# Fewer, wider band matmuls, another order of the first loads, and the third conv slot moved to the stage border

## The chip, the cores and the metric

The kernel runs on one core of one Trainium2 chip. The time is device microseconds of one execution; the figure for the kernel before is the median of three executions, 521.17 us (521.16 to 522.0). Engines are named as in the profile: PE (TensorE, matmuls), PEld (its weight loads), DVE (VectorE), ACT (ScalarE), POOL (GpSimd), SP (SyncE, which here only issues transfers). POOL and SP each issue transfers from a list of their own, in program order; ACT can issue some too.

## The reference

A causal depthwise convolution of seven taps, whose weights are a softmax over the taps and differ per head (8 heads of 24 channels), is followed by a gated feed-forward block. Cut to what is computed:

```python
# x: (8, 3904, 192) float32, weight: (8, 7)
w = softmax(weight, axis=-1)                       # (sum + 1e-9 below)
x_pad = concatenate([zeros((B, 6, D)), x], axis=1)
out = einsum('hk,bskhg->bshg', w, windows_of_7(x_pad))
x = out.reshape(31232, 192)
a, b = x @ w1, x @ w2                              # 192 -> 1024
h = (a * b) @ w3                                   # 1024 -> 1024
return h @ w_out                                   # 1024 -> 192, float32
```

Nothing nonlinear stands between `w3` and `w_out`, so the kernel multiplies these two once and uses the product `W_sb` (1024 x 192).

## The kernel before, in words

**Tokens.** The 31,232 tokens are two streams (r = 0 and 1) of 15,616, which lie on partitions 0 to 63 and 64 to 127. The convolution works on windows of 64 input rows that give 58 output rows. Windows are grouped in 12 blocks (`SIZES`: 6, 4, 8, 10, 8, six of 36, and 20 windows). The feed-forward part works on 31 rounds R of 512 tokens per stream, in groups of four rounds.

**Convolution.** A head's seven taps become a banded 64 x 64 matrix. `band` (L245) builds the bands: DVE multiplies shifted diagonals by the tap weights (L247, tile `cprod`), PE sums the seven products through an identity (L256), and ACT or DVE casts the sum to `Aband` (`put`, L479). One call makes the bands of one head pair for both streams. `conv` (L274) then takes, for each head, four 64 x 64 matmuls (two halves of the block by two streams, L290) and casts the result to `convo` (L311, or L476 through `move` in the opening).

**First product.** `first_part` (L403) makes one part of 128 of the 1024 columns: a factor a by `wd[0]` and a factor b by `wd[1]` (six matmuls each, L381, 64 rows by 128 columns of the array, one per stream), an ACT cast of a to `asb` (L389), and a DVE multiply of `asb` by b into `abT` (L400). **Second product** (L420): 32 matmuls per round and stream (L432), a cast to `osb` (ACT, L437), and an output store.

**PSUM.** Four pairs of banks go round through the list `free`: `banks()` takes the first, `drained(p)` appends it behind the copy that empties it. So every PE result waits until the pair that it gets has been emptied.

**Order.** The program is scheduled by hand: each engine runs its instructions in the order in which the source writes them. After the opening come the four first products of group 0 with the small blocks' convolutions between them, then the product of `w3` and `w_out` (L467), and then for every group the eight second products, followed by the four first products of the next group. In each stage of second products one block is convolved, in three slots (heads 0 to 2, 3 to 5, 6 and 7) that stand behind the second products with index 1, 3 and 5 (4, 5 and 6 in the first stage, where block 5 has the slots 0, 1 and 2). The last slot also issues the block's store to `rows` in DRAM on SP; SP's transposes (L363) later bring these rows back as `xT`.

**The opening.** SP loads the first quarter of both weights as float32 into `wfirst` (L164), and ACT and POOL cast it into the two partition halves of `wd` (`cast_w`). The other quarters are loaded by POOL with a cast on the way (`load_w`, L169) and copied to the upper half by POOL (`copy_w`, L190). POOL's list begins with block 0's x for stream 0 (L172), two selects that make the diagonal `diag` (L176), block 0's x for stream 1, block 0's first rows (L182), block 1's x (L119), and the second quarter of the weights. ACT issues the load of the tap weights `wall` (L137).

**The pace.** In front of block 5's and 6's x loads POOL copies two elements of `w3T` into a scratch tile `pace` (L557). The copy waits for one of the transposes that bring `w3` in, and so it holds back all that POOL issues behind it.

Of the kernel before, what the change touches and what calls it, by code (L numbers as in the profile page):

```python
# [8 lines left out]
FP32 = mybir.dt.float32  # L9
BF16 = mybir.dt.bfloat16  # L10
AX = mybir.AxisListType
ALU = mybir.AluOpType
# [4 lines left out]
def kernel(  # L17
# [10 lines left out]
    nc = tc.nc  # L28

    B, S, D = x.shape  # L30
    H, K = weight.shape
    G = D // H
    DFF = moe_w1.shape[1]
    JT = DFF // 128
# [6 lines left out]
    GROUP = 4  # L41
    RING = GROUP * CH
    Q = 64
    ST = Q - PAD
    NP = D // Q
# [5 lines left out]
    NB = len(SIZES)  # L51
# [10 lines left out]
    work = ctx.enter_context(tc.tile_pool(name="work", bufs=2))  # L62
# [6 lines left out]
    free = list(range(NPAIR))  # L69
# [12 lines left out]
    def slot(shape, dtype, name):  # L82
        return stage.tile(shape, dtype, tag="slot", bufs=5, name=name)
# [21 lines left out]
    def load_x(b, parts=(0, 1)):  # L105
        tiles = xb_of.setdefault(b, [])
        zeros_of = zero_rows.setdefault(b, [])
        for i0, n in [v for e, v in enumerate(halves_of(b)) if e in parts]:
            xb = work.tile([128, n, D], BF16, tag="xb", bufs=5, name="xb")
            w = 0  # L110
            while w < n:
                i = i0 + w
                m = min(n - w, WB - i % WB)
                at_end = i + m == NWIN
                if at_end:
                    m -= 1
                if m:
                    for r in range(NS):
                        nc.gpsimd.dma_start(out=xb[Q * r:Q * r + Q, w:w + m, :],  # L119
                                            in_=x_spans(r, i, m))  # L120
                if i % WB == 0:
                    zeros_of += [(xb, 0, w), (xb, 1, w)]
                w += m
                if at_end:
                    nc.gpsimd.memset(xb[Q:128, w, :], 0.0)
                    t = tok(NWIN - 1) - PAD
                    nc.gpsimd.dma_start(out=xb[0:Q, w, :], in_=x_rows[t:t + Q, :])
                    nc.gpsimd.dma_start(out=xb[Q:Q + PAD + LAST, w, :],
                                        in_=x_rows[TS + t:TS + t + PAD + LAST, :])
                    w += 1  # L130
            if len(halves_of(b)) == 1:
                tiles += [(xb, 0), (xb, SIZES[b] // 2)]
            else:
                tiles.append((xb, 0))

    wall = const.tile([1, H, K], FP32)
    nc.scalar.dma_start(out=wall, in_=weight.rearrange("(o h) k -> o h k", o=1))  # L137

    n0 = SIZES[0] // 2
    xb0 = work.tile([128, 2 * n0, D], BF16, tag="xb", bufs=5, name="xb")  # L140
    xb_of[0] = [(xb0, 0), (xb0, n0)]
    wfirst = work.tile([Q, 2, NP, DFF // 4], FP32, tag="abT", bufs=GROUP, name="wfirst")
    pace = const.tile([1, 2], BF16)
    tiny = const.tile([128, 1], FP32)
    ones = const.tile([128, 1], BF16)
    zeros = const.tile([128, 128], BF16)
    half = const.tile([1, 3 * Q], BF16)
    ident = const.tile([128, 128], BF16)
    diag = const.tile([128, Q + PAD], BF16)
    nc.vector.memset(zeros, 0.0)  # L150
    nc.vector.memset(tiny, 0.0)
    nc.vector.memset(ones, 1.0)  # L152
    nc.vector.memset(xb0[:, 0, :], 0.0)
    nc.vector.memset(half, 0.0)
    nc.vector.memset(half[:, Q:2 * Q], 1.0)
# [3 lines left out]
    WC = (0, DFF // 4, DFF // 2, DFF * 3 // 4, DFF)  # L159
    wd = [const.tile([128, NP, DFF], BF16, name=f"wd{i}", tag=f"wd{i}") for i in range(2)]  # L160
    w_rows = [w.rearrange("(k q) f -> q k f", q=Q) for w in (moe_w1, moe_w2)]

    for i in range(2):
        nc.sync.dma_start(out=wfirst[:, i], in_=w_rows[i][:, :, 0:WC[1]])  # L164

    def load_w(part):
        cs = slice(WC[part], WC[part + 1])
        for i in range(2):
            nc.gpsimd.dma_start(out=wd[i][0:Q, :, cs], in_=w_rows[i][:, :, cs])  # L169

    def load_x0(r):
        nc.gpsimd.dma_start(out=xb0[Q * r:Q * r + Q, 1:, :], in_=x_spans(r, 1, 2 * n0 - 1))  # L172

    load_x0(0)
    for p0 in (0, Q):
        nc.gpsimd.affine_select(  # L176
            out=diag[p0:p0 + Q], in_=ones[p0:p0 + Q].to_broadcast([Q, Q + PAD]),
            pattern=[[-1, Q + PAD]], compare_op=ALU.is_equal, fill=0.0, base=0,
            channel_multiplier=1)
    load_x0(1)  # L180
    for r in range(NS):
        nc.gpsimd.dma_start(out=xb0[Q * r + PAD:Q * r + Q, 0, :],  # L182
                            in_=x_rows[r * TS:r * TS + ST, :])
    load_x(1)
    def cast_w(i, r, f):
        f(out=wd[i][Q * r:Q * r + Q, :, 0:WC[1]], in_=wfirst[:, i])

    def copy_w(part, i, f):
        cs = slice(WC[part], WC[part + 1])
        f(out=wd[i][Q:128, :, cs], in_=wd[i][0:Q, :, cs])  # L190

    load_w(1)
    cast_w(1, 1, nc.gpsimd.tensor_copy)
    load_w(2)
    load_x(2)
    for i in range(2):
        copy_w(1, i, nc.gpsimd.tensor_copy)
# [5 lines left out]
    def warm(n):  # L203
        p, t = banks()
        for j in range(n):
            nc.tensor.matmul(t[:, j % 2, :], zeros, zeros[:, 0:1].to_broadcast([128, CH]),  # L206
                             start=True, stop=True)
        drained(p)

    warm(6)  # L210

    wmax = const.tile([1, H], FP32)
    wsum = const.tile([1, H], FP32)
# [1 line left out]
    wsb = const.tile([128, 2, 2, K], BF16)  # L215
    nc.vector.reduce_max(out=wmax, in_=wall, axis=AX.X)
    nc.vector.tensor_tensor(
        out=wall, in0=wall, in1=wmax.unsqueeze(2).to_broadcast([1, H, K]), op=ALU.subtract)
# [5 lines left out]
        out=wrow, in0=wall, in1=wsum.unsqueeze(2).to_broadcast([1, H, K]), op=ALU.mult)  # L224
# [11 lines left out]
    Aband = const.tile([128, 2, 2, 2, Q], BF16)  # L236

    def band_of(h, r):
        return Aband[Q * r:Q * r + Q, h // 4, (h % 4) // 2, int(h % 2 != r), :]

    d0 = diag[:, 0:1]
    taps = bass.AP(tensor=d0.tensor, offset=d0.offset,
                   ap=[list(d0.ap[0]), [1, K], [1, Q]])

    def band(g, e):  # L245
        c = slot([128, K, Q], BF16, "cprod")
        nc.vector.tensor_tensor(  # L247
            out=c, in0=taps, in1=wsb[:, g, e].unsqueeze(2).to_broadcast([128, K, Q]),
            op=ALU.mult)
        p, bps = banks()  # L250
        for k in range(K):
            for v in range(2):
                for r in range(2):
                    rs = slice(Q * r, Q * r + Q)
                    o = Q * (r ^ v)
                    nc.tensor.matmul(bps[o:o + Q, v, 0:Q], ident[rs, rs], c[rs, k, :],  # L256
                                     start=(k == 0), stop=(k == K - 1))
        return p, Aband[:, g, e], bps[:, :, 0:Q]


    xT = [const.tile([128, RING + Q], BF16, name=f"xT{k}", tag=f"xT{k}") for k in range(NP)]

# [140 lines left out]
    def first_part(R, fts, c0, c1):  # L403
        a, b = (first_factor(R, i, fts, c0, c1) for i in range(2))
        first_times(R, fts, c0, c1, first_cast(*a), *b)
# [1 line left out]
    def first_tile(R):  # L407
        abT_of[R] = work.tile([128, JT, NS, CH], BF16, tag="abT", bufs=GROUP, name="abT")

    def first_product(R, between=None, fts=range(JT)):  # L410
        if R not in abT_of:
            first_tile(R)
        N = width(R)
        step = CH // N
        for ft in fts[::step]:
            first_part(R, list(range(ft, ft + step)), 0, N)
            if between and ft in between:
                between[ft]()

# [33 lines left out]
    w3T = const.tile([128, JT, DFF], BF16)  # L453
# [24 lines left out]
    def put(f, p, dst, src):  # L478
        f(out=dst, in_=src)  # L479
        drained(p)  # L480

    cast_w(0, 0, A)
    put(A, *band(0, 0))
    put(A, *band(0, 1))
    cast_w(0, 1, A)
    made = [band(1, 0), band(1, 1)]
    put(V, *made[0])
    put(V, *made[1])
    cast_w(1, 0, A)

    def move_all(p, moves, fs):
        for f, m in zip(fs, moves):
# [41 lines left out]
    def need(R):  # L534
        return next(i for i in range(NWIN) if tok(i) >= (R + 1) * CH)
# [18 lines left out]
        3: seq([(pe_transposes, 4)])})  # L554
    store(4, need(GROUP - 1) - 1, queue=nc.gpsimd)
    nc.gpsimd.dma_start(out=wo_b, in_=wor)
    P(out=pace, in_=w3T[0:1, JT // 2 - 1, DFF - 2:DFF])  # L557
    load_x(5)
    load_x(6)
    first_product(3)  # L560
# [11 lines left out]
    slots = (range(0, 3), range(3, 6), range(6, H))  # L572
# [6 lines left out]
    for p, rounds in enumerate(groups):  # L579
        b = PROLOGUE_BLOCKS + p  # L580
        order = rounds[-1:] + rounds[:-1] if rounds[-1] == NR - 1 else rounds
        for j, R in enumerate(order if p else ()):
            first_product(R)
            send(R + GROUP)
            if j < 2 and b < NB:
                P(out=pace, in_=abT_of[R][0:1, JT - 1, 1, 0:2])  # L586
                load_x(b, (j,))
        if b < NB:
            zero(b)
        at = {1: [(b, slots[0])], 3: [(b, slots[1])], 5: [(b, slots[2])]}  # L590
        if p == 0:
            at = {0: [(5, slots[0], (V, A))], 1: [(5, slots[1], (V, A))],
                  2: [(5, slots[2], (V, A), need(GROUP))], 4: at[1], 5: at[3], 6: at[5]}
        for i, (R, r) in enumerate((R, r) for R in rounds for r in range(NS)):
            second_product(R, r, R == NR - 1 and r == 1, nc.sync if p else nc.gpsimd)
            for c in at.get(i, ()) if b < NB else ():
                conv_heads(*c)
            if p == 0 and i == 2:
                send(2 * GROUP - 1)
# [31 lines left out]
```

## Time and profile before

| | us |
|---|---|
| median of three executions | 521.17 |
| the profiled execution | 522.07 |
| its span, first to last instruction | 520.4 |
| PE busy | 513.5 (99%) |
| DVE busy | 357.5 (69%) |
| ACT busy | 325.7 (63%) |
| POOL busy | 58.4 (11%) |
| granted TensorE clock, mean over the span | 1.000 |

The span is shorter than the execution's time, because the profile counts from the first to the last instruction of the program. The rows of the profile read: start and length in us (timeline and chain), engine, line of the kernel, operation, output<-inputs, shapes, and in brackets the idle time of the engine ahead of the row and what ended it. "SPq" or "ACTq" is an engine's issuing side, which does not count as busy. The chain is followed back from the last instruction; each piece of it is either work or the wait for what released the next piece.

### The profile page before, as it was taken

How to read it: one execution, taken by the hardware profiler on the slowest of the kernel's cores; microseconds unless marked ns; L12 is line 12 of the kernel's file. 1: busy time of each engine (PE TensorE's matmuls, PEld its weight loads, DVE VectorE, ACT ScalarE, POOL GpSimd, SP SyncE). 2: the span in 40 equal slices, each digit the busy share in tenths (PEclk: the TensorE clock that was granted, in tenths of full speed). 3: DMA queues.
4: the chain of work that ended last, by engine and by line, in shares of the span. 5: the costliest groups of instructions: out<-in, count | busy, mean ns of one | idle time of the engine just before them, and what ended most of it. 6: DMA issues, size and time to landing. Idle time of an engine off the chain costs nothing.

```text
span 520.4 us, 13006 instructions
## 1 busy us (share of the span) xinstructions
PE 513.5 (99%) x5576; PEld 339.8 (65%) x5576; DVE 357.5 (69%) x343; ACT 325.7 (63%) x410; POOL 58.4 (11%) x98
## 2 busy tenths in 40 slices
PE   8999999999999999999999999999999999999997
PEld 4455788455885558845588455884558855599567
DVE  6778646899538994389943899438993299911970
ACT  6887643777437774377743777337774377734762
POOL 8501522130000200002000010001200000000000
PEclk9999999999999999999999999999999999999999
DMA  9979998699656973569645699456724532024004
GB/s 116 169 142 126 163 222 208 162 186 166 143 146 161 116 94 113 146 161 128 82 116 147 155 122 89 118 146 157 103 44 122 155 96 32 17 94 151 1 3 152
DMA packets 133420, 64.61 MB, mean 124 GB/s; under 512 B 90304, under 2 KB 132642, under 8 KB 133298
## 3 DMA queue, kind: packets, MB, share of 16 engines
q1 hardware_dynamic: 94320, 44.06, 36.1%
q0 software_dynamic: 38896, 19.62, 30.4%
q8 instruction: 43, 0.70, 0.6%
q14 instruction: 15, 0.12, 0.1%
q10 hardware_dynamic: 146, 0.10, 0.1%
HBM read 33.25 MB, written 36.52 MB: 134 GB/s over the span
## 4 chain that ended last, share of the span: by engine, by line
PE 95%; ACT 1%; DVE 1%; DMA 1%; POOL 1%; issue 0%; POOLq 0%; ACTq 0%
PE pairs L381 59%; PE pairs L432 32%; PE pairs L290 3%; DVE abT L400 1%; PE pairs L467 1%; ACT asb L389 1%; DMA xb<-in_x_dram 1%; PE pairs L343 0%; POOL xb L172 0%; POOL xb L182 0%; ACT convo L311 0%; POOL xb L119 0%; ACT xT L355 0%; POOL diag L176 0%; PE pairs L507 0%
## 5 line engine op out<-in xcount | busy, mean ns | idle before, releaser
L400 DVE TENSOR_TENSOR abT<-asb,pairs 128x1024 bf16<-128x1024 bf16 (+1 forms) x245 | 298.1, 1217 | 76.8 <-ACT asb L389 60.5
L381 PE MATMUL pairs<-xT,wd 64*128 64x512 bf16 (+3 forms) x3000 | 319.7, 371 | 0.7 <-DVE abT L400 0.3
L389 ACT CAST asb<-pairs 128x1024 bf16<-128x1024 f32 (+1 forms) x245 | 247.1, 1009 | 67.7 <-PE pairs L381 67.3
L381 PEld LDWEIGHTS <-wd 64*128 64x128 bf16 x3000 | 162.3, 94 | 151.8 <-issue 1.8
L432 PE MATMUL pairs<-W_sb,abT 128*128 128x192 bf16 x1952 | 166.1, 246 | 0.0
L432 PEld LDWEIGHTS <-abT 128*128 128x128 bf16 x1952 | 159.6, 98 | 9.7 <-issue 9.7
L437 ACT COPY osb<-pairs 128x384 f32<-128x384 f32 x122 | 58.3, 478 | 116.0 <-PE pairs L432 116.0
L311 DVE CAST convo<-pairs 128x864 bf16<-128x864 f32 (+5 forms) x67 | 50.8, 815 | 67.6 <-PE pairs L290 67.6
L119 POOL DMA_DIRECT2D xb<-in_x_dram x42 | 32.2, 781 | 7.6 <-PE pairs L381 4.1
L586 POOL COPY pace<-abT 1x2 bf16<-1x2 bf16 x10 | 1.7, 174 | 238.7 <-DVE abT L400 238.7
L290 PE MATMUL pairs<-xb,Aband 64*64 64x432 bf16 (+5 forms) x384 | 17.5, 284 | 0.4 <-DMA xb<-in_x_dram 0.3
L290 PEld LDWEIGHTS <-Aband 64*64 64x64 bf16 x384 | 7.2, 106 | 7.5 <-issue 6.3
L311 ACT CAST convo<-pairs 128x512 bf16<-128x512 f32 (+4 forms) x15 | 8.1, 584 | 0.5 <-PE pairs L290 0.4
L444 POOL DMA_DIRECT2D out_dram<-osb x8 | 6.1, 758 | 18.4 <-ACT osb L437 18.4
L437 DVE COPY osb<-pairs 128x192 f32<-128x192 f32 x1 | 0.4, 358 | 11.1 <-PE pairs L432 11.1
L467 PEld LDWEIGHTS <-w3T 128*128 128x128 bf16 x64 | 5.2, 98 | 0.4 <-issue 0.4
L467 PE MATMUL pairs<-wo_b,w3T 128*128 128x192 bf16 x64 | 5.5, 246 | 0.0
L190 POOL COPY wd<-wd 64x768 bf16<-64x768 bf16 x6 | 4.8, 847 | 0.0
L206 PE MATMUL pairs<-zeros 128*128 128x512 bf16 x8 | 3.7, 615 | 1.1 <-DVE ones L152 1.1
L343 PE MATMUL pairs<-ident,convo 128*128 128x128 bf16 x48 | 3.9, 219 | 0.7 <-DVE convo L476 0.5
L343 PEld LDWEIGHTS <-convo 128*128 128x128 bf16 x48 | 2.9, 97 | 2.5 <-issue 1.6
L469 ACT CAST W_sb<-pairs 128x192 bf16<-128x192 f32 x8 | 2.6, 320 | 2.8 <-PE pairs L467 2.8
(52 smaller groups left out, 38.6 us busy)
## 6 DMA issues: line engine op xcount, KB each, us to landing
out_dram<-osb SPq DMA_DIRECT2D x52, 384.0 KB
xb<-in_x_dram POOLq DMA_DIRECT2D x18, 432.0 KB, 7.8
rows<-convo SPq DMA_DIRECT2D x8, 648.0 KB
out_dram<-osb POOLq DMA_DIRECT2D x8, 384.0 KB, 4.9
w3rows<-in_moe_w_dram POOLq DMA_DIRECT2D x2, 1024.0 KB, 12.0
xb<-in_x_dram POOLq DMA_DIRECT2D x6, 240.0 KB, 5.4
rows<-convo SPq DMA_DIRECT2D x4, 324.0 KB
xT<-rows SPq DMA_TRANSPOSE x81
```

What stands on the lines that cost most here:

```text
L119: nc.gpsimd.dma_start(out=xb[Q * r:Q * r + Q, w:w + m, :], in_=x_spans(r, i, m))
L190: f(out=wd[i][Q:128, :, cs], in_=wd[i][0:Q, :, cs])
L290: nc.tensor.matmul(view(slice(Q * c, Q * c + Q), r)[:, :, j * G:(j + 1) * G], band_of(h, r), xb[Q * r:Q * r + Q, w0:w0 + n, h * G:(h + 1) ...
L311: f[e % len(f)](out=dst, in_=part)
L343: nc.tensor.transpose(out=tps[:, w, :], in_=convo[:, w, k].rearrange("p r g -> p (r g)"), identity=ident)
L381: nc.tensor.matmul(p[:, r, e * n:e * n + n], wd[i][rs, k, ft * 128:(ft + 1) * 128], xT[k][rs, r0 + c0:r0 + c1], start=(k == 0), stop=(k == ...
L389: nc.scalar.copy(out=asb, in_=pa)
L400: nc.vector.tensor_tensor(out=dst, in0=asb, in1=pb, op=ALU.mult)
L432: nc.tensor.matmul(ops[:, (g - g0) * D:(g - g0) * D + D], ab[:, jt, r, g * 128:(g + 1) * 128], W_sb[:, jt, :], start=(jt == 0), stop=(jt = ...
L437: f(out=osb[:, g0:g0 + per, :].rearrange("p g d -> p (g d)"), in_=ops[:, 0:per * D])
L444: queue.dma_start(out=out[t0:t0 + ng * 128, :].rearrange("(g p) d -> p g d", p=128), in_=osb)
L467: nc.tensor.matmul(wps[:, 0, 0:D], w3T[:, gt, jt * 128:(jt + 1) * 128], wo_b[:, gt, :], start=(gt == 0), stop=(gt == JT - 1))
```

## The change

- **Bands.** `bands(g)` takes the place of two calls of `band(g, e)`: two DVE multiplies write the two head pairs side by side into one `cprod` tile, and each of the 28 matmuls has 128 columns instead of 64. There are 56 such matmuls instead of 112, and two casts of 256 elements (one on ACT, one on DVE) instead of four of 128. `Aband`'s axes change their order to suit.
- **First loads.** SP loads the tap weights and then the first quarter of the first weight alone. The second weight's first quarter is loaded by POOL with a cast, behind block 0's x and ahead of block 1's; POOL copies it to the upper half behind the issues of the second and third quarters. POOL's cast and one ACT cast go.
- **Selects.** POOL sets `ones` itself and runs the selects ahead of all its loads. One of six warm-up matmuls goes.
- **Pace.** The copy that holds block 5's x reads what the second transpose of `w3`'s second half brings, not the fourth.
- **Border.** In the stages of second products the third slot stands behind index 7, the last one, instead of index 5 (6 in the first stage), and its two heads are cast by DVE and ACT, one each, instead of both by DVE. In the first product behind such a border, two entries of `free` are exchanged behind the second part.

```diff
-    nc.scalar.dma_start(out=wall, in_=weight.rearrange("(o h) k -> o h k", o=1))
+    nc.sync.dma_start(out=wall, in_=weight.rearrange("(o h) k -> o h k", o=1))
...
-    wfirst = work.tile([Q, 2, NP, DFF // 4], FP32, tag="abT", bufs=GROUP, name="wfirst")
+    wfirst = work.tile([Q, NP, DFF // 4], FP32, tag="abT", bufs=GROUP, name="wfirst")
...
-    nc.vector.memset(ones, 1.0)
...
-    for i in range(2):
-        nc.sync.dma_start(out=wfirst[:, i], in_=w_rows[i][:, :, 0:WC[1]])
+    nc.sync.dma_start(out=wfirst, in_=w_rows[0][:, :, 0:WC[1]])
...
-    load_x0(0)
+    nc.gpsimd.memset(ones, 1.0)
     for p0 in (0, Q):
         nc.gpsimd.affine_select(
...
+    load_x0(0)
     load_x0(1)
     for r in range(NS):
         nc.gpsimd.dma_start(out=xb0[Q * r + PAD:Q * r + Q, 0, :],
                             in_=x_rows[r * TS:r * TS + ST, :])
+    load_w(0, (1,))
     load_x(1)
...
     load_w(1)
-    cast_w(1, 1, nc.gpsimd.tensor_copy)
     load_w(2)
+    copy_w(0, 1, nc.gpsimd.tensor_copy)
     load_x(2)
...
-    warm(6)
+    warm(5)
...
-    def band(g, e):
-        c = slot([128, K, Q], BF16, "cprod")
-        nc.vector.tensor_tensor(
-            out=c, in0=taps, in1=wsb[:, g, e].unsqueeze(2).to_broadcast([128, K, Q]),
-            op=ALU.mult)
+    def bands(g):
+        c = slot([128, K, 2, Q], BF16, "cprod")
+        for e in range(2):
+            nc.vector.tensor_tensor(
+                out=c[:, :, e, :], in0=taps,
+                in1=wsb[:, g, e].unsqueeze(2).to_broadcast([128, K, Q]), op=ALU.mult)
...
-                    nc.tensor.matmul(bps[o:o + Q, v, 0:Q], ident[rs, rs], c[rs, k, :],
+                    nc.tensor.matmul(bps[o:o + Q, v, 0:2 * Q], ident[rs, rs],
+                                     c[rs, k].rearrange("p e s -> p (e s)"),
                                      start=(k == 0), stop=(k == K - 1))
...
-    def first_product(R, between=None, fts=range(JT)):
+    def first_product(R, between=None, fts=range(JT), behind_conv=False):
...
             first_part(R, list(range(ft, ft + step)), 0, N)
+            if behind_conv and ft == step:
+                free[1], free[2] = free[2], free[1]
...
-    cast_w(0, 0, A)
-    put(A, *band(0, 0))
-    put(A, *band(0, 1))
-    cast_w(0, 1, A)
-    made = [band(1, 0), band(1, 1)]
-    put(V, *made[0])
-    put(V, *made[1])
-    cast_w(1, 0, A)
+    A(out=wd[0][0:Q, :, 0:WC[1]], in_=wfirst)
+    put(A, *bands(0))
+    A(out=wd[0][Q:128, :, 0:WC[1]], in_=wfirst)
+    put(V, *bands(1))
...
-    P(out=pace, in_=w3T[0:1, JT // 2 - 1, DFF - 2:DFF])
+    P(out=pace, in_=w3T[0:1, 1, DFF - 2:DFF])
...
-            first_product(R)
+            first_product(R, behind_conv=j == 0 and b <= NB)
...
-        at = {1: [(b, slots[0])], 3: [(b, slots[1])], 5: [(b, slots[2])]}
+        at = {1: [(b, slots[0])], 3: [(b, slots[1])], 7: [(b, slots[2], (V, A))]}
         if p == 0:
             at = {0: [(5, slots[0], (V, A))], 1: [(5, slots[1], (V, A))],
-                  2: [(5, slots[2], (V, A), need(GROUP))], 4: at[1], 5: at[3], 6: at[5]}
+                  2: [(5, slots[2], (V, A), need(GROUP))], 4: at[1], 5: at[3], 7: at[7]}
```

More of the change, by code (lines that the diff above doesn't have):

```diff
@@ L161, with load_w @@
     w_rows = [w.rearrange("(k q) f -> q k f", q=Q) for w in (moe_w1, moe_w2)]
-    for i in range(2):
-        nc.sync.dma_start(out=wfirst[:, i], in_=w_rows[i][:, :, 0:WC[1]])
-    def load_w(part):
+    nc.sync.dma_start(out=wfirst, in_=w_rows[0][:, :, 0:WC[1]])
+    def load_w(part, which=(0, 1)):
         cs = slice(WC[part], WC[part + 1])
-        for i in range(2):
+        for i in which:
             nc.gpsimd.dma_start(out=wd[i][0:Q, :, cs], in_=w_rows[i][:, :, cs])
@@ L183 @@
                             in_=x_rows[r * TS:r * TS + ST, :])
+    load_w(0, (1,))
     load_x(1)
-    def cast_w(i, r, f):
-        f(out=wd[i][Q * r:Q * r + Q, :, 0:WC[1]], in_=wfirst[:, i])
     def copy_w(part, i, f):
@@ L238, in band_of @@
     def band_of(h, r):
-        return Aband[Q * r:Q * r + Q, h // 4, (h % 4) // 2, int(h % 2 != r), :]
+        return Aband[Q * r:Q * r + Q, h // 4, int(h % 2 != r), (h % 4) // 2, :]
     d0 = diag[:, 0:1]
@@ L255, in band @@
                     o = Q * (r ^ v)
-                    nc.tensor.matmul(bps[o:o + Q, v, 0:Q], ident[rs, rs], c[rs, k, :],
+                    nc.tensor.matmul(bps[o:o + Q, v, 0:2 * Q], ident[rs, rs],
+                                     c[rs, k].rearrange("p e s -> p (e s)"),
                                      start=(k == 0), stop=(k == K - 1))
-        return p, Aband[:, g, e], bps[:, :, 0:Q]
+        return p, Aband[:, g].rearrange("p v e s -> p v (e s)"), bps[:, :, 0:2 * Q]
     xT = [const.tile([128, RING + Q], BF16, name=f"xT{k}", tag=f"xT{k}") for k in range(NP)]
```

## The prediction
> **What bounds the kernel now.** I read the page's busy line first, then the chain of work that ended last, then the timeline of the three places that the change touches: the opening, the end of the first weight stage, and a border between two stages.
>
> ```profile
> span 520.4 us, 13006 instructions
> PE 513.5 (99%) x5576; PEld 339.8 (65%) x5576; DVE 357.5 (69%) x343; ACT 325.7 (63%) x410; POOL 58.4 (11%) x98
> ...
> L400 DVE TENSOR_TENSOR abT<-asb,pairs 128x1024 bf16<-128x1024 bf16 (+1 forms) x245 | 298.1, 1217 | 76.8 <-ACT asb L389 60.5
> ```
>
> TensorE (PE) is busy for all but 6.9 us, so only stalls, tile switches and the opening can be won. The profiled execution took 522.07 us (span 520.4 and 1.67 around it); the median of the runs is 521.17, so I add my sum to that median. The chain, in order of time:
>
> ```profile
> 5.19 4.20 DMA xb<-in_x_dram
> 9.39 0.04 issue
> 9.43 0.44 PE pairs L290 x31
> ...
> 67.44 0.30 PE pairs L290 x3
> 67.74 0.01 issue
> 67.75 0.70 PE pairs L290 x9
> 68.46 2.75 PE pairs L432 x32
> 71.20 0.67 PE pairs L290 x12
> ...
> 149.62 0.49 PE pairs L290 x8
> 150.10 5.39 PE pairs L432 x64
> 155.49 41.55 PE pairs L381 x384
> ```
>
> Before 9.39 the chain is POOL's list of DMA issues and then the landing of block 1's second x load; from 9.43 on it is PE. Block 5's first conv slot took 0.30 + 0.01 + 0.70 = 1.01 us where the same 12 matmuls took 0.67: a stall of 0.34.
>
> **The opening.** Its timeline:
>
> ```profile
> 0.81 0.51 ACTq L137 DMA_DIRECT2D wall<-in_weight_dram  x1
> 0.90 0.11 DVE L150 MEMSET zeros<- 128x64 uint32 x1 [0.90 <-PEq L615]
> 1.32 0.85 POOL L172 DMA_DIRECT2D xb<-in_x_dram  x1 [0.80 <-POOLq L615]
> 2.26 0.59 POOL L176 TENSOR_SCALAR_AFFINE_SELECT diag<-ones 64x70 bf16<-64x70 bf16 x2
> 2.79 0.71 POOL L172 DMA_DIRECT2D xb<-in_x_dram  x1
> 3.50 1.09 POOL L182 DMA_DIRECT2D xb<-in_x_dram  x2
> 4.23 2.23 DVE L247 TENSOR_TENSOR cprod<-diag,wsb 128x448 bf16<-128x448 bf16 x4
> 4.57 1.27 POOL L119 DMA_DIRECT2D xb<-in_x_dram  x2
> 5.81 1.28 POOL L169 DMA_DIRECT2D wd<-in_moe_w_dram  x2
> 6.99 0.29 DVE L479 CAST Aband<-pairs 128x128 bf16<-128x128 f32 x1 [0.24 <-PE pairs L256]
> 7.13 0.82 POOL L186 CAST wd<-wfirst 64x768 bf16<-64x768 f32 x1
> 8.92 0.21 PE L290 MATMUL pairs<-xb,Aband 64*64 64x48 bf16 x1
> ```
>
> PE had conv(1) ready at 8.92 and stood until 9.43 for x. So what counts is when block 1's second load is issued and how long it takes.
>
> POOL's list up to the end of that issue. Before: from 1.32 to 4.57 + 1.27 = 5.84. After: the new memset of `ones` (some 0.1, as DVE's memset row), selects 0.59, block 0's x 0.85 + 0.71, its row parts 1.09, the new weight load 1.28 / 2 = 0.64, block 1's x 1.27: 5.25 us. The selects are no DMA, so they may start when DVE did (0.90) or only when POOL did (1.32). The issue then ends at 6.15 to 6.57, 0.31 to 0.73 later; I take 0.35, nearer to DVE's start, because the 0.80 of idle time stands before a DMA and not before a compute instruction.
>
> The time to landing (windows of POOL's issues to `xb`: first the two row parts of block 0, then block 1's second load):
>
> ```profile
> DMA to landing us min/median/max: 3.0/3.2/3.3
> ...
> DMA to landing us min/median/max: 4.2/4.2/4.2
> ```
>
> The 4.2 holds a backlog of about 1 us over the 3.2. SP's second `wfirst` transfer (192 KB) leaves SP's queue, and as many bytes of the source now stand ahead of block 1 in POOL's queue, so I keep the 4.2 and give the change 0.05 for the freed engines: conv(1) starts 0.3 later. Low end: with 3.2 x would land before PE is ready, and PE's own chain decides, 9.43 - 9.15 = 0.3 sooner (next paragraph). High end: 0.73, and 0.1 for more backlog, 0.8 later.
>
> [...]
>
> [...]
>
> PE's side. The bands were 112 matmuls of 64 columns behind four multiplies; now 56 of 128 columns behind the second and the fourth. The last multiply still ends at 4.23 + 2.23 = 6.46; the last group was done at 6.99, 0.53 later. Twice the columns cost between 0 and 0.3 more, and one cast of 256 elements between 0.29 (128) and 0.58 (two of them): the second half of conv(0) comes 0.1 to 0.4 later, conv(1) is ready at 9.0 to 9.3 instead of 8.92. I take 9.15. That is hidden under x; without the cover it would cost 0.2. ACT loses one cast of the first weights and the issue of `wall` (0.51), which goes in front of `wfirst` on SP; the first cast comes up to 0.5 later, and the work behind it, the first band's cast, waits for the second multiply (5.4) and PE anyway: nothing.
>
> POOL's later list. The cast at 7.13 goes; four weight issues (2 x 1.28) and a copy of the same size (0.82) follow block 1: 6.19 + 2.56 + 0.82 = 9.57. `wd[1]`'s upper half is read by the second factor of the first part, which PE reaches at about 9.7 + 0.44 + 0.5 = 10.6: hidden by 1.0. Block 2's x is issued from 9.57 on instead of some 9.2 (7.13 + 0.82 + 1.28), and all later copies and loads, the w3 loads too, slip 0.4 with PE slipping 0.3. Opening: +0.3.
>
> **The pace.** Block 5's x is held by a POOL copy that reads `w3T`.
>
> ```profile
> 51.22 0.17 POOL L557 COPY pace<-w3T 1x2 bf16<-1x2 bf16 x1 [9.60 <-DMA w3T<-w3rows]
> 51.75 7.17 POOL L119 DMA_DIRECT2D xb<-in_x_dram  x9 [0.36 <-PE pairs L381]
> 59.34 5.45 PE L467 MATMUL pairs<-wo_b,w3T 128*128 128x192 bf16 x64
> 67.45 0.25 POOL L564 MEMSET xb<- 6x192 bf16 x1 [0.34 <-DMA xb<-in_x_dram]
> ```
>
> The stall at 67.74 ends when POOL's memset, at 67.45, is through (67.70). The copy now waits for the second transpose of w3's second half, not the fourth. Two transposes earlier is between 0 (a queue that empties at once) and 2 x 1.3; I take 1.0. With the opening's 0.3 to 0.4 on both sides, the memset ends near 67.0 while PE arrives near 67.7: the stall of 0.34 goes. Next late there is nothing nearer than 0.6. Bounds: 0 to -0.34. The price on the other side: the loads meet more of the transposes, whose last must be in when the fifth w3 product ends (59.34 + 5 x 0.68 = 62.7); that is a rival.
>
> **The border.** For each of blocks 6 to 11 the third slot (two heads, 8 matmuls) moves behind the stage's last second product, just ahead of the next first product; head 6 is evicted by DVE and head 7 by ACT. Block 5's third slot already has this form:
>
> ```profile
> 74.55 0.56 PE L290 MATMUL pairs<-xb,Aband 64*64 64x432 bf16 x8
> 74.66 0.48 ACT L437 COPY osb<-pairs 128x384 f32<-128x384 f32 x1 [0.84 <-PE pairs L432]
> 74.98 1.06 DVE L311 CAST convo<-pairs 128x864 bf16<-128x864 f32 x1 [1.33 <-PE pairs L290]
> 75.19 0.88 ACT L311 CAST convo<-pairs 128x864 bf16<-128x864 f32 x1
> ...
> 155.42 16.80 PE L381 MATMUL pairs<-xT,wd 64*128 64x512 bf16 x154
> 156.29 1.01 ACT L389 CAST asb<-pairs 128x1024 bf16<-128x1024 f32 x1 [0.28 <-PE pairs L381]
> 157.39 15.41 DVE L400 TENSOR_TENSOR abT<-asb,pairs 128x1024 bf16<-128x1024 bf16 x12 [5.39 <-ACT asb L389]
> 157.58 1.01 ACT L389 CAST asb<-pairs 128x1024 bf16<-128x1024 f32 x1 [0.28 <-PE pairs L381]
> ```
>
> What it saves: 12 matmuls take 0.67 and 8 take 0.49, so a head is 0.18 and a slot has 0.13 fixed, for two changes of tile shape. The border has one change already: 41.55 less 32 parts of 1.295 (157.58 - 156.29) is 0.11. A slot at the border makes two where there were three in all, so it saves about 0.1: 6 x 0.095 = 0.57 at the most.
>
> What it costs: let L be the start of the first product, 0.49 behind the slot. ACT's cast of head 7 then runs from L + 0.15 to L + 1.03, where the first `asb` cast stood at L + 0.87: that cast is 0.17 late. DVE's first multiply (1.22 by L400's mean) starts at L + 1.97 + 0.17 = 2.14 and ends at 3.36, the second at 4.58. The pairs of banks go round, four of them: the third part's second factor (L + 0.65 + 2.59 = 3.24) would wait for the first multiply; the new exchange in `free` gives it the pair of the second cast, ready at 3.17. The fourth part's second factor (L + 4.54) needs the second multiply, 4.58 plus some 0.05 of issue: a stall of 0.09, and by the fifth part DVE, 0.075 a part faster than PE, has caught up. Net for five blocks of 36 windows: 0.095 - 0.09, nothing; block 11 is shorter and keeps 0.095. I take -0.15 in all, between -0.57 and +0.3. SP: the rows' stores now stand behind the last two output stores and start some 5 us later; the transposes behind them are wanted a whole stage later, so nothing waits.
>
> **Sum:** +0.3 - 0.34 - 0.15 = -0.2, a median of 521.0 us, which no measurement here tells from no change: 0.2% is 1.04 us.
>
> **Rivals.**
> - *Early x* (the freed SP queue empties the backlog): opening -0.3, stall -0.34, border clean -0.57: -1.2, 520.0. For it: 1 us of backlog in the 4.2. Against: the bytes ahead of block 1 are the same. 0.2. [...]
> - *Late w3T, slower than before*: the x loads, released sooner, delay the last transpose past 62.7 + 0.3, and the fifth w3 product waits. From that point each us counts in full; 1.5 us late gives 522.3, and the end, if it waits until x is through at 67.45, would be 4.5 us. For it: the pace stands there at all. Against: no wait at L467 shows now, and the loads move only 1 us. 0.12.
> - *The border stalls*: if the exchange does not help, both second factors wait, 0.17 and 0.13 at each border, and one further part after that 0.1: 6 x (0.4 - 0.095) = +1.8; with the rest 522.8. 0.1.
> - *It does nothing*: the stall at block 5 stays, the opening is level: 521.2. 0.08.
>
> **How the numbers follow.** The forecast holds 0.5. Faster by over 0.2%: early x and a tail of the forecast, 0.21. Slower: late w3T, the border, a tail of a late opening, 0.23. Within: 0.56. The likeliest case's own range is 520.4 to 521.8; 519.8 to 522.4 takes in early x and the nearer part of the slow cases.
>
> **What would show it.** Conv(1)'s first full run near 9.7 (opening right), below 9.3 (early x), above 10.2 (wrong). Block 5's first slot at 0.67 in the chain. After each border 41.55 plus nothing or 0.1 for L381, and no slot of 0.49 inside a stage of second products. L467 at 5.39. A wait of PE for DVE in the fourth part after a border shows the late multiply. A span that changes by over 1 us with these in place makes the prediction wrong.

## The result, and the profile after

The changed kernel takes 523.01 us (median of 17 executions, 521.77 to 524.58); the kernel before, measured beside it, 521.73 us (17 executions, 521.16 to 523.11). The ratio is 1.0026, with a 95% interval of 1.0017 to 1.0035: slower by about 1.3 us. The prediction of 521.0 us (519.8 to 522.4) missed, and by its sign. The profiled execution of after took 522.78 us against 522.07 of before, so the pair of traces holds 0.71 of these 1.3 us. One execution of all those reported here, of 1894 us in the run b2 below, is left out of its ratio.

The page of after, its busy line:

```profile
span 521.1 us, 12901 instructions
PE 514.3 (99%) x5519; PEld 340.5 (65%) x5519; DVE 351.4 (67%) x335; ACT 329.3 (63%) x414; POOL 59.2 (11%) x100
```

PE issues 57 matmuls fewer than before (5519 against 5576) and is busy 0.8 us longer (514.3 against 513.5). So the loss is in how long matmuls take, not in waits. Where, the chain of work shows (start, length in us; engine, output and line). Numbers of lines have moved by the edit: L289 is what L290 was, L342 L343, L380 L381, L433 L432, L468 L467, L504 L507. After:

```profile
8.24 1.30 PE pairs L342 x9
9.54 0.56 PE pairs L289 x23
10.09 1.85 PE pairs L380 x12
11.95 0.76 PE pairs L504 x6
12.70 3.80 PE pairs L380 x54
...
60.72 5.39 PE pairs L468 x64
...
68.75 0.67 PE pairs L289 x12
...
91.42 10.90 PE pairs L380 x100
102.32 0.02 issue
...
156.44 41.55 PE pairs L380 x384
...
517.31 0.32 ACT osb L438
```

The rows of before that answer to them, as far as the prediction did not show them:

```profile
9.87 0.99 PE pairs L381 x12
10.86 0.44 PE pairs L507 x6
11.30 3.89 PE pairs L381 x54
...
59.41 5.39 PE pairs L467 x64
...
90.57 41.55 PE pairs L381 x384
```

How far after lies behind before at the same piece of work:

| at | after − before, us | what happened since the row above |
|---|---|---|
| first part's second half (L380 x54) | 12.70 − 11.30 = +1.40 | the opening |
| product of `w3` and `w_out` | 60.72 − 59.41 = +1.31 | |
| first stage of first products behind block 5 | 91.42 − 90.57 = +0.85 | block 5's stall (0.34) gone, one border |
| second products behind that stage | 133.17 − 132.11 = +1.06 | a wait at 102.32 which before did not have, some 0.2 |
| next stage of first products | 156.44 − 155.49 = +0.95 | one border, 0.11 |
| the last copy | 517.31 − 516.79 = +0.52 | four more borders |

(132.11 and 516.79 are the starts of these pieces in the chain of before, 133.17 in that of after.) The whole loss arises between 8 and 13 us. There the same twelve matmuls of the first part take 1.85 us in after and 0.99 in before, the six transposes of L504 0.76 against 0.44. They compute the same on the same tiles. What differs is PE's clock: the trace's record of the granted clock goes to full at 4.61 us in before and at 12.61 us in after. (The view by windows prints 1.00 where no transition is on record yet, and so hides this; the durations show it.) From 12.61 us on, a row of after takes what the same row of before takes, within 0.1 us, but for the places that the table names.

### The profile page after: what moved, and what is told of

Its sections match the earlier page's. It is cut to its first block, busy times and chain, and to the rows that moved or that the text cites. A ratio compares the mean times of both kernels' runs of the same rounds, so it can differ in the third digit from the quotient of the medians.

```text
span 521.1 us, 12901 instructions
## 1 busy us (share of the span) xinstructions
PE 514.3 (99%) x5519; PEld 340.5 (65%) x5519; DVE 351.4 (67%) x335; ACT 329.3 (63%) x414; POOL 59.2 (11%) x100
## 4 chain that ended last, share of the span: by engine, by line
PE 95%; DVE 2%; ACT 1%; DMA 0%; issue 0%; ACTq 0%
PE pairs L380 59%; PE pairs L433 31%; PE pairs L289 3%; DVE abT L399 1%; PE pairs L468 1%; ACT asb L388 1%; PE pairs L342 1%; DVE cprod L246 0%; DMA wall<-in_weight_dram 0%; PE pairs L255 0%; ACT convo L310 0%; PE pairs L504 0%; ACT xT L354 0%; DVE Aband L480 0%; ACT osb L438 0%
## 5 line engine op out<-in xcount | busy, mean ns | idle before, releaser
L380 PE MATMUL pairs<-xT,wd 64*128 64x512 bf16 (+3 forms) x3000 | 320.6, 372 | 0.7 <-DVE abT L399 0.2
L380 PEld LDWEIGHTS <-wd 64*128 64x128 bf16 x3000 | 162.0, 94 | 153.8 <-issue 3.3
L433 PEld LDWEIGHTS <-abT 128*128 128x128 bf16 x1952 | 159.9, 98 | 7.8 <-issue 7.8
L433 PE MATMUL pairs<-W_sb,abT 128*128 128x192 bf16 x1952 | 165.0, 246 | 0.0
L310 DVE CAST convo<-pairs 128x864 bf16<-128x864 f32 (+5 forms) x61 | 45.4, 798 | 96.7 <-PE pairs L289 92.5
L289 PE MATMUL pairs<-xb,Aband 64*64 64x432 bf16 (+5 forms) x384 | 17.5, 292 | 0.3 <-DVE Aband L480 0.3
L310 ACT CAST convo<-pairs 128x864 bf16<-128x864 f32 (+5 forms) x21 | 13.1, 653 | 0.4
L289 PEld LDWEIGHTS <-Aband 64*64 64x64 bf16 x384 | 7.3, 113 | 7.3 <-issue 6.0
L468 PEld LDWEIGHTS <-w3T 128*128 128x128 bf16 x64 | 5.2, 98 | 0.4 <-issue 0.4
L468 PE MATMUL pairs<-wo_b,w3T 128*128 128x192 bf16 x64 | 5.5, 246 | 0.0
L342 PE MATMUL pairs<-ident,convo 128*128 128x128 bf16 x48 | 4.4, 235 | 0.1
L342 PEld LDWEIGHTS <-convo 128*128 128x128 bf16 x48 | 3.1, 102 | 2.1 <-issue 1.5
L167 POOL DMA_DIRECT2D wd<-in_moe_w_dram x7 | 4.4, 646 | 0.0
```

The costliest lines, as they stand in the source:

```text
L289: nc.tensor.matmul(view(slice(Q * c, Q * c + Q), r)[:, :, j * G:(j + 1) * G], band_of(h, r), xb[Q * r:Q * r + Q, w0:w0 + n, h * G:(h + 1) ...
L310: f[e % len(f)](out=dst, in_=part)
L342: nc.tensor.transpose(out=tps[:, w, :], in_=convo[:, w, k].rearrange("p r g -> p (r g)"), identity=ident)
L380: nc.tensor.matmul(p[:, r, e * n:e * n + n], wd[i][rs, k, ft * 128:(ft + 1) * 128], xT[k][rs, r0 + c0:r0 + c1], start=(k == 0), stop=(k == ...
L433: nc.tensor.matmul(ops[:, (g - g0) * D:(g - g0) * D + D], ab[:, jt, r, g * 128:(g + 1) * 128], W_sb[:, jt, :], start=(jt == 0), stop=(jt = ...
L468: nc.tensor.matmul(wps[:, 0, 0:D], w3T[:, gt, jt * 128:(jt + 1) * 128], wo_b[:, gt, :], start=(gt == 0), stop=(gt == JT - 1))
```

## The experiments

Theory A: the wide bands leave PE without work for longer while DVE multiplies, PE's clock comes up late or falls back, and the opening is run at half rate. The rival, B: the loss has a cause outside the clock, in the order of the first loads or in the longer chain of dependent work in front of block 1's convolution, which matmuls that compute nothing can't cure. Beside them stood the question whether the border gains at all (C: it does not). None of the kernels leaves computation out. Each was compared with the kernel before on the same chip; the medians of before were 521.89, 522.09 and 521.72 us in the three groups a, b and c (a run's letter is its group's).

### The warm-up matmuls

**After with the sixth warm-up matmul back (a1):**

```diff
-    warm(5)
+    warm(6)
```

> The changed kernel with six warm-up matmuls instead of five. [...] Theory B (the wide bands' own longer chain makes the opening late, the warm-up matmul is worth nothing): within 0.3 us of the changed kernel, as the sixth matmul only takes 0.4 us.

Measured: 522.94 us, ratio 1.0019 (1.0005 to 1.0032), so nearly all of the loss is still there. Its windows (first column: stretch; then its length, then busy us and count of PE, PEld, DVE, ACT, POOL; then the granted clock, the DMA share and GB/s):

```profile
5.10:8.40 3.30, 2.00 (x91) 1.46 (x90) 2.51 (x6) 2.35 (x5) 3.30 (x6) 1.00 1.12 117
8.50:11.80 3.30, 3.30 (x53) 1.83 (x54) 1.25 (x4) 1.87 (x4) 3.26 (x5) 0.50 1.02 120
```

The clock came up at 5.05 us and, after a stretch in which PE was busy for 2.00 of 3.30 us, went back to half for 3.41 us. The twelve matmuls of the first part take 1.85 us again. So the missing warm-up matmul is not the cause by itself, and theory A failed here in its number: it had put the median 0.5 to 1.4 us below after, with the clock up before 8 us. The number is the one that B had given, and only the profile shows that the clock was lost all the same.

**Before with one warm-up matmul less (a2):**

```diff
-    warm(6)
+    warm(5)
```

> The kernel before with five warm-up matmuls instead of six, nothing else. [...] Theory B: within 0.2 us.

Measured: 522.1 us, ratio 1.0004 (0.9987 to 1.0022). Taken alone, the removal costs nothing that shows; in its profile the twelve matmuls take 0.99 us, from 9.39. Theory A had left open 0.5 to 1.5 us above before or within 0.3 of it, B had said within 0.2, so this run does not part them.

**After with more warm-up in front of the bands** (six, and four instead of two behind `wsb`, where PE waits for the first two multiplies; a4):

```diff
-    warm(5)
+    warm(6)
...
-    warm(2)
+    warm(4)
```

> The changed kernel with six warm-up matmuls ahead and four instead of two behind the tap weights' matmul, so that the PE has work from 1.07 us until the first band. Theory A: the clock rises near 4.5 to 7 us in nearly all executions; the best of the four, 1.2 to 2.0 us below the changed kernel, and 0.3 to 0.9 us below the kernel before. Theory B: 0 to 0.3 us above the changed kernel, as the bands wait for the added matmuls.

Measured: 521.52 us, ratio 0.9996 (0.9983 to 1.0009). Three matmuls that compute nothing take about 1.5 us off the changed kernel. Its chain:

```profile
9.10 0.37 PE pairs L289 x32
9.47 0.99 PE pairs L380 x12
10.46 0.44 PE pairs L504 x6
10.90 3.89 PE pairs L380 x54
```

The first part is back at 0.99, at full clock from 4.51 us on. B can't explain this: the loads and the dependent work are those of after.

**The same kernel once more (c4)**, beside the third group:

> The changed kernel with 6 + 4 warm-up matmuls once more, on the chip of this call, as the measure for the other three. Theory A: 521.2 to 521.9, below the kernel before of this call, as in the first call. Theory B: at the changed kernel's 523.

Measured: 521.6 us, ratio 0.9994 (0.9982 to 1.0006), the same. But its profile caught an execution in which the cure failed:

```profile
6.50:9.80 3.30, 2.37 (x78) 1.48 (x71) 1.77 (x5) 2.35 (x5) 3.26 (x6) 1.00 1.12 118
9.90:13.20 3.30, 2.91 (x48) 1.73 (x48) 0.88 (x2) 1.22 (x2) 3.20 (x6) 0.50 1.17 133
```

Here block 1's x landed at 10.24 us, PE stood waiting for it, and the clock fell back from 9.86 to 13.27. So the clock differs between executions of one kernel. A fall of 3.41 us to half lowers the mean granted clock of an execution to about 0.997 (half of 3.41 us is 0.33% of 520; the profiled executions have 0.997 in c4 and a1, and 0.993 in b1, whose fall lasted 6.83 us). Of the executions on record, 5 of 12 have 0.997 or less with the wide bands alone (b1 below), 3 of 17 in after, 3 of 12 each in a1 and a3, 1 of 35 in a4, c1 and c4 together, and 10 of 107 in the kernel before beside them. A late rise, such as that in the profile of after, does not show in this mean, so how often the clock comes up late stays open.

**Before with the longer second warm-up (c3):**

```diff
-    warm(2)
+    warm(4)
```

> The kernel before with four instead of two matmuls behind the tap weights' matmul, nothing else. Theory A: its narrow bands leave smaller holes, but part of its executions get the clock late too, so 0 to 0.5 us below the kernel before, mostly at the upper end. Theory B: 0.1 to 0.4 us above it, as the first band waits for two half-rate matmuls.

Measured: 522.66 us, ratio 1.0011 (1.0 to 1.0021). More warm-up does not help the kernel before, whose clock was up at 4.61 us already; its own profile has the twelve matmuls at 0.99 us, from 9.90, and block 5's stall (0.48) is still there. Both theories had put it nearer to before. Its profiled execution, the longest of the twelve, also has PE waiting 0.73 us for the last transpose of `w3` at 63.49 us, with the pace of before.

### The wide bands

**After with the narrow bands of before (a3)** (five warm-up matmuls, all else as in after; the function `band` comes back with its 64 columns):

```diff
-    put(A, *bands(0))
+    put(A, *band(0, 0))
+    put(A, *band(0, 1))
...
-    put(V, *bands(1))
+    made = [band(1, 0), band(1, 1)]
+    put(V, *made[0])
+    put(V, *made[1])
```

> The changed kernel with the old narrow bands (four groups of 28 matmuls of 64 columns, one behind each multiply) and five warm-up matmuls. Theory A: the hole in front of the bands closes from 0.7 to about 0.2 us, so the clock rises sooner in part of the executions: 0.3 to 1.2 us below the changed kernel. Theory B: 0.3 to 0.6 below it, from the shorter chain to the second half of block 0's convolution, whatever the clock does.

Measured: 522.08 us, ratio 1.0012 (0.9995 to 1.0029); in its profile the clock is full from 4.41 us and the twelve matmuls take 0.99. It is 0.9 us under after, but the intervals overlap, and in this execution x landed at 9.95. By itself it does not decide; the next one does.

**Before with the wide bands and nothing else of the change (b1)** (`bands` and the order of `Aband`'s axes are those of after):

```diff
-    put(A, *band(0, 0))
-    put(A, *band(0, 1))
+    put(A, *bands(0))
...
-    put(V, *made[0])
-    put(V, *made[1])
+    put(V, *bands(1))
```

> The kernel before with the wide bands alone (two groups of 28 matmuls of 128 columns, each behind two multiplies; six warm-up matmuls, old loads, old border). [...] Theory B (only the chain to block 0's second half is longer, and it is hidden under block 1's x): within 0.3 us of the kernel before.

Measured: 523.44 us, ratio 1.0023 (1.0009 to 1.0037). The wide bands alone, with all six warm-up matmuls, the old loads, the old pace and the old border, cost as much as the whole change does. Its windows:

```profile
3.80:7.10 3.30, 1.88 (x66) 1.27 (x69) 2.52 (x6) 1.85 (x3) 3.29 (x6) 1.00 1.21 155
7.20:13.90 6.70, 6.50 (x102) 3.66 (x98) 3.39 (x8) 4.20 (x10) 6.70 (x10) 0.50 1.18 136
14.00:17.00 3.00, 3.00 (x48) 1.81 (x46) 1.84 (x3) 2.02 (x3) 3.00 (x6) 1.00 0.64 70
```

Full clock while PE has work for 1.88 of 3.30 us, then half rate for 6.83 us (7.12 to 13.95), in which PE is busy nearly throughout. That is theory A in one view, and the 1.35 us between the medians lie in the 0.6 to 1.4 that A had given. In front of the two groups of bands PE has nothing for 0.93 and 0.49 us there, by its timeline. In the kernel before, with the narrow bands, PE has more to do in the stretch that follows the rise of its clock:

```profile
4.61:8.02 3.41, 2.50 (x145) 1.81 (x144) 2.92 (x8) 3.00 (x7) 3.37 (x6) 1.00 1.20 130
```

2.50 of 3.41 us, against 1.99 in b1 over as long a stretch from its rise, 2.06 in a1, and 2.31 in a4, where the two fillers stand.

**Narrow bands and the longer warm-up, with the rest of the change (b3):**

```diff
     # narrow bands as above
-    warm(5)
+    warm(6)
...
-    warm(2)
+    warm(4)
```

> The changed kernel with narrow bands and 6 + 4 warm-up matmuls. Theory A: the PE has no hole over 0.2 us from 1.07 us to block 0's convolution, so the clock rises near 4.5 us in nearly all executions and stays: 521.0 to 521.6, at or below the wide bands with 6 + 4. Theory B: 0.3 to 0.6 us below the wide bands with 6 + 4, by the shorter chain.

Measured: 521.36 us, ratio 0.9991 (0.9978 to 1.0003), the lowest median of group b; 1 of its 12 executions has a mean granted clock of 0.997 or less. But the profiled execution, with a span of 521.5, shows a wait that after does not have, in its chain (L466 is the product of `w3` and `w_out` here):

```profile
54.09 10.19 DMA w3T<-w3rows
...
64.33 2.24 PE pairs L466 x25
```

The last transpose of `w3`, issued with the x loads under way, took 10.19 us, and PE waited for it for 1.27 us. That is the wait of the prediction's rival *late w3T*; but c3 has it too, 0.73 us with the old pace, so that the sooner x loads make it is not shown.

### The border and the pace

**The kernel with the longer warm-up (a4), the border undone (b2):**

```diff
-            first_product(R, behind_conv=j == 0 and b <= NB)
+            first_product(R)
...
-        at = {1: [(b, slots[0])], 3: [(b, slots[1])], 7: [(b, slots[2], (V, A))]}
+        at = {1: [(b, slots[0])], 3: [(b, slots[1])], 5: [(b, slots[2])]}
...
-                  2: [(5, slots[2], (V, A), need(GROUP))], 4: at[1], 5: at[3], 7: at[7]}
+                  2: [(5, slots[2], (V, A), need(GROUP))], 4: at[1], 5: at[3], 6: at[5]}
```

> The changed kernel with 6 + 4 warm-up matmuls and the third slot back inside the stage (index 5, index 6 in the first stage, both heads on DVE, no exchange in free). Theory A: the border is worth 6 x 0.095 = 0.57 us without any stall, so this is 0.4 to 0.6 us slower than the same kernel with the border (521.5), level with the kernel before. Theory C (the border gains nothing, as the prediction had it, a stall of 0.09 against 0.095): within 0.15 us of it.

Measured: 521.6 us, ratio 0.9988 (0.9979 to 0.9997). By the medians, 521.6 against a4's 521.52 in another group, C would hold; but medians of so few executions can't show 0.5 us. The chain can, because behind the opening its rows repeat to a hundredth. A stage with the border undone, from one block of first products to the next:

```profile
89.82 41.55 PE pairs L380 x384
...
149.35 5.38 PE pairs L433 x64
154.74 41.55 PE pairs L380 x384
```

And with the border (a4):

```profile
89.79 41.55 PE pairs L380 x384
...
154.12 0.49 PE pairs L289 x8
154.61 41.55 PE pairs L380 x384
```

154.74 − 89.82 = 64.92 against 154.61 − 89.79 = 64.82: 0.10 a block, and neither has a wait behind the border. From block 5's first slot to the start of the last copy it is 449.07 against 448.45 us: 0.62, which is 0.10 for each of the six borders. (To the end of the span it is 452.72 against 452.21, 0.51; behind the last copy a4 took 0.11 longer.) So C falls; the border gains the whole 0.095 that the prediction had worked out, and no stall eats it. That it is the change of tile shape which costs the 0.10 is the author's estimate from the 0.67 and 0.49 us of the slots.

**a4 with the pace of before (b4):**

```diff
-    P(out=pace, in_=w3T[0:1, 1, DFF - 2:DFF])
+    P(out=pace, in_=w3T[0:1, JT // 2 - 1, DFF - 2:DFF])
```

> The changed kernel with 6 + 4 warm-up matmuls and the pace on the fourth transpose of the second half, as before. If the pace is what took the stall at block 5's first slot away: the stall of 0.3 to 0.6 us is back in the chain and the median is that much above 521.5. If the stall went with the sooner opening of POOL's list: the slot takes 0.67 and the median stays within 0.15 us.

Measured: 522.26 us, ratio 1.0002 (0.9992 to 1.0012), with block 5's stall back in the chain:

```profile
67.66 0.26 POOL xb L561
...
67.96 0.70 PE pairs L289 x9
```

Block 5's first slot, from its first matmul to its last, takes 0.98 us here and 0.40 in a4: 0.58 of stall. The stall is there in four of the five profiles with the old pace (all but b1, where PE comes to the slot only at 69.59), and in none of the nine with an earlier one; in some of these, after among them, PE comes to the slot more than 1 us later than in a4, so that the clean pair is this one, b4 against a4.

**a4 with the pace one transpose later than after's (c1):**

```diff
-    P(out=pace, in_=w3T[0:1, 1, DFF - 2:DFF])
+    P(out=pace, in_=w3T[0:1, 2, DFF - 2:DFF])
```

> The changed kernel with 6 + 4 warm-up matmuls and the pace on the third transpose of the second half, between the two versions. If the loads released by the second transpose now and then hold up the last transpose of w3 (one profile had 1.6 us of it): fewer late executions and a median within 0.2 us of the same kernel with the second transpose. If the third is too late for block 5: 0.2 to 0.4 us above it.

Measured: 521.1 us (520.92 to 521.78), ratio 0.9984 (0.9975 to 0.9993), 0.6 us under before and 0.42% under after by the two ratios. With b2 (0.9988) it is one of the two whose interval lies wholly under the kernel before. In its chain:

```profile
9.47 0.99 PE pairs L380 x12
...
67.04 0.67 PE pairs L289 x12
```

The clock holds, block 5 has no stall (POOL's memset behind its x starts at 64.18), no wait follows a border. Against a4 in the same group (0.9994, 0.9982 to 1.0006) the intervals overlap, so that the later pace itself is the gain is not shown.

**The narrow kernel (b3) with that pace (c2):**

```diff
-    P(out=pace, in_=w3T[0:1, 1, DFF - 2:DFF])
+    P(out=pace, in_=w3T[0:1, 2, DFF - 2:DFF])
```

> Narrow bands, 6 + 4 warm-up matmuls, pace on the third transpose, border and loads as changed. Theory A, with the w3 transposes no longer held up: the fastest of all, 521.0 to 521.5, with no execution above 522.5. Theory B: 0.3 to 0.6 us below the wide bands of the same call.

Measured: 521.59 us (521.06 to 523.98), ratio 1.0001 (0.9989 to 1.0012), so it is not the fastest of all. Its profile has both of the waits that remain, `w3`'s last transpose and, in the first stage behind block 5, the transposes of x rows:

```profile
54.26 9.49 DMA w3T<-w3rows
...
99.56 2.74 DMA xT<-rows
```

PE waits 0.89 us for the first of them. What makes the last transpose late stays open: it was late in two of the nine profiles with an earlier pace (b3 and c2) and in one of the five with the old one (c3). These three are the profiles of kernels with narrow bands and the longer second warm-up, and none of the other eleven has the wait; one profile of each can't tell whether that is chance. What makes the wait near 102 us (0.2 us in after; also in b1, b3, b4, c3 and c4) was not tried; b1 and c3 have it with the old border and the old pace.

## Why the prediction was wrong

Wrong was the opening, and there the sentence on the bands: "That is hidden under x; without the cover it would cost 0.2." It counted the columns and the casts of the wide bands and never asked at what clock PE runs them. The opening cost +1.40 in the pair of profiles where +0.3 was forecast, and against a4, with the same bands and loads at full clock, it cost 12.70 − 10.90 = 1.80; b1 shows the loss from the bands alone (+0.23%, where the prediction had nothing), and a4 takes it away. The rows that could have raised the question were quoted already: the 4.23 + 2.23 of DVE's multiplies, during which the narrow bands gave PE four pieces of work and the wide ones give it two. PE's rows of after there:

```profile
3.68 1.03 PE L204 MATMUL pairs<-zeros 128*128 128x512 bf16 x2
5.21 2.03 PE L255 MATMUL pairs<-cprod,ident 64*64 64x128 bf16 x56 [0.51 <-DVE cprod L246]
...
7.77 0.45 PE L289 MATMUL pairs<-xb,Aband 64*64 64x72 bf16 x16 [0.29 <-DVE Aband L480]
```

PE has nothing for 0.51 us in front of the bands, where before stood only from 4.83 to 4.91, and 0.29 behind them. The columns themselves were costed well: at full clock (a4) conv(1) starts at 9.10, for the 9.15 of the prediction. And the sign that was to show the opening right, conv(1) near 9.7, did appear (9.54): it looked at where the work starts, not at how fast it then runs. The other signs came as well (block 5's slot at 0.67, L468 at 5.39, 41.55 behind the borders but the first), and the time was wrong all the same. None of the rivals named the clock.

**x of block 1.** Predicted: 0.3 later. POOL's list went as said in its parts, but started sooner:

```profile
0.81 0.10 POOL L172 MEMSET ones<- 128x1 bf16 x1 [0.29 <-POOLq L612]
0.99 0.54 POOL L174 TENSOR_SCALAR_AFFINE_SELECT diag<-ones 64x70 bf16<-64x70 bf16 x2
1.48 1.59 POOL L170 DMA_DIRECT2D xb<-in_x_dram  x2
...
4.76 1.30 POOL L119 DMA_DIRECT2D xb<-in_x_dram  x2
```

The issue ended at 6.06 against 5.84, 0.22 later for 0.35. Yet x landed at 8.82, where before had 9.39. The step that failed is to read 4.2 us of landing as a property of the queue: it is a draw. With the new order of loads x landed at 8.82 (after), 9.38 (b4), 9.95 (a3) and 10.24 (c4), and in a4, b2 and c1 by 9.10, where PE begins conv(1) without a wait; with the old order at 9.39 (before) and 9.42 (c3), and in a2 by 9.02. With this scatter a single pair of traces can't show 0.3. And with x at 8.82 the cover under which the bands were hidden was gone as well: conv(1) starts at 9.54 behind PE's own chain.

**The pace.** Right in its mechanism: POOL's rows at block 5,

```profile
49.46 0.18 POOL L554 COPY pace<-w3T 1x2 bf16<-1x2 bf16 x1 [6.53 <-DMA w3T<-w3rows]
...
65.29 0.25 POOL L561 MEMSET xb<- 6x192 bf16 x1 [0.23 <-DMA xb<-in_x_dram]
```

The copy stands 1.76 us sooner (49.46 for 51.22; 1.0 was taken, between 0 and 2.6), the memset 2.16 sooner, and block 5's first slot is at 0.67 in one piece. In after itself this proves little: PE came to the slot at 68.67, behind the 67.70 at which the memset of before was through. b4 against a4 shows it, 0.58 for the 0.34. The rival *late w3T* did not happen in after (L468 took 5.39). The wait exists, at the place named (1.27 us in b3, 0.89 in c2), but c3 has it without the earlier pace, so that the rival's cause is not shown.

**The border.** Mis-sized, on the good side: −0.15 was taken, 0.62 was measured up to the last copy (b2), a little over the −0.57 given as the most. The timeline of after:

```profile
156.37 4.06 PE L380 MATMUL pairs<-xT,wd 64*128 64x512 bf16 x36
156.54 0.88 ACT L310 CAST convo<-pairs 128x864 bf16<-128x864 f32 x1
157.32 1.02 ACT L388 CAST asb<-pairs 128x1024 bf16<-128x1024 f32 x1
158.42 2.37 DVE L399 TENSOR_TENSOR abT<-asb,pairs 128x1024 bf16<-128x1024 bf16 x2 [0.99 <-ACT asb L388]
```

With L = 156.37, ACT's first `asb` cast starts at L + 0.95, where before had 156.29 − 155.42 = 0.87: it is 0.08 late, not 0.17. ACT starts it 0.10 before the row of its 0.88 us cast ends (157.42). DVE is through with two multiplies at 160.79 = L + 4.42, for the 4.58 of the prediction, and the fourth part's second factor at L + 4.54 need not wait. So the stall of 0.09 that ate up the gain does not come, and the rival in which the border stalls has no support in any run. (Two slips of the working change nothing here: the rows 156.29 and 157.58 give 1.29 a part, not 1.295, and with it the border's own 0.11 would be 0.27, so these rows could not show it; and the price of the stalling border, with the rest, comes to 522.9, not 522.8.)

**The sum.** Of the pair: +1.40 in the opening, −0.09 up to the product of `w3` and `w_out`, −0.34 at block 5, −0.66 at the six borders, +0.21 at 102.3, which is the +0.52 at the last copy; behind it after takes 0.18 longer to the end of its span. That is +0.70, with +0.71 measured between the two profiled executions. The medians are 1.28 us apart; the profiled execution of before lay above its median (522.07 over 521.73) and that of after below (522.78 under 523.01). Where the longer warm-up mends the clock and all else stays (a4, c4), the ratios lie 0.04% and 0.06% under before, 0.2 to 0.3 us and not clear of zero. That is near the forecast −0.2, but by luck, as its terms are not those measured: the border alone gained 0.62 for 0.15.

## What to carry to other kernels

A stretch in which PE waits anyway was not free here: in b1 PE was busy for 1.99 of 3.41 us, the clock then fell to half for 6.83 us, and the kernel took 0.23% longer. So ahead of an edit that gathers matmuls into fewer, later groups near the start of a kernel, look at when the granted clock rises and how much work PE keeps in the stretch behind. Here three matmuls that compute nothing were worth the whole loss, some 1.5 us (a4). A landing time from one profile is a draw (8.82 us in after, 10.24 in c4); take it from several before a step of 0.3 us rests on it, and compare chains piece by piece, because gains of 0.1 us a stage show there and not in medians.

## What the runs showed of the hardware

- The granted clock came up at different times: at 3.71 us in b1, 4.41 in a3, 4.51 in a4, 4.61 in before, 5.05 in a1, 5.18 in c1, 6.44 in c4 and 12.61 in after. It fell back to half for 3.41 us in a1 (8.47 to 11.88) and c4 (9.86 to 13.27) and for 6.83 us in b1 (7.12 to 13.95). Twelve matmuls of 348 columns took 1.85 us at half (after), 0.99 at full (before). The falls came behind stretches in which PE had work: it was busy for 2.06 of 3.42 us (a1), 1.99 of 3.41 (b1) and 2.43 of 3.42 (c4).
- The busy share alone does not tell which way it goes: c4 fell behind its 2.43 of 3.42 us, a3 kept full clock through a stretch with 2.23 of 3.41. For the rise it is the same: in after the clock did not come up behind 3.41 us with PE busy for 3.00, but behind the next stretch, with 3.42 of 3.42; in c4 it came back behind 2.98 of 3.41. What decides it stays open.
- The landing of block 1's x scattered by 1.4 us between executions (8.82 in after, 10.24 in c4) with the same order of loads ahead of it.
- At the five borders behind blocks of 36 windows in after, ACT's next instruction starts 0.10 us before the row of the one before it ends (157.32 against 157.42 at the one shown above, where the first `asb` cast is so 0.08 us late, not the 0.17 of the prediction).
